# Attention with a gated FFN: new due times and engines for the first pair's rotary steps

## The chip, the cores and the metric

The kernel runs on one core of a Trainium2 chip. The metric is device time in microseconds (us) of one execution. Five engines matter here: TensorE (PE in the profile, with PEld for its weight loads), VectorE (DVE), ScalarE (ACT), GpSimd (POOL) and SyncE (SP), which here only issues DMAs. Each engine works through its own instructions strictly in the order in which the program lists them.

## The reference, cut to what matters

q, k and v have 8 batches, 8 heads, 576 positions and 64 features, all float32.

```python
q_rot, k_rot = rotate(q), rotate(k)        # x1*cos - x2*sin, x1*sin + x2*cos
scores = scale * q_rot @ k_rot.T           # scale = 1/8
attn = exp(scores - max) / (sum + 1e-9)
x = (attn @ v) with the heads side by side # (8, 576, 512)
gate = sigmoid(causal 5-tap convolution of x, one filter per channel)
out = (gate * (x @ w_val)) @ w_out
```

## The kernel before

The work goes by pairs of heads, 32 pairs in all. The host lays q and k out as [pair, 128, 2, 576]: 128 partitions are two heads of 64 features, the middle axis holds the features and the features with their halves swapped. With a table of cosines and signed sines in the same layout (`tab`, two planes), the rotation of a pair is two multiplications (`rope_mul`, plane 0 and plane 1, L211) and an addition (`rope_add`, L215). The result is then split into a rounded high part (`qk_hi`, a copy on ScalarE, L222) and a low part (`qk_lo`, a subtraction, L226), because the score matmuls (`s_mm`, L254) form each product from three partial products. Scores go to PSUM (three buffers), `s_max` (VectorE, L260) takes the row maximum and `s_exp` (ScalarE, L273) the exponential; transposes, the product with v, the convolution and, for every four pairs, the FFN follow.

The first pair alone is cut along the positions: the keys into 0 to 287 (steps with suffix `_0`) and 288 to 575 (`_1`), the queries into 0 to 255 (`_0`) and 256 to 575 (`_1`). The table is loaded in two halves on ScalarE's DMA queue (`ltab`) and each half is multiplied in place by the root of the score scale (`stab`, ScalarE, L207). The halves of k and q are loaded on SP's queue (`loadk`, `loadq`). `k_front` (ScalarE, L189) copies the last 64 keys, which lie in key half `_1`, in front of the first; every score matmul of a pair but the very first instruction comes behind it.

The convolution weights (`taps`) and the FFN weights arrive as 64-bit patterns and are decoded on the chip. `load_weight` brings four chunks of w_val (`lval0` to `lval3`, 512 KB each) on SP's queue; the decode of a chunk (`dval`) begins on VectorE with the TENSOR_SCALAR of L488.

The order of everything is written by a planner. Each step is added as a job with a due time (a base written in the code plus the entry of `DUE` under the step's key), an engine (`PICK` where there is a choice: V VectorE, G GpSimd, A ScalarE), and the names that it reads and writes. `Plan.order` takes the jobs off a heap, always the one with the lowest due time among those whose predecessors are already placed; a job whose rotating buffer is not yet free in the order is put off until the buffer's last user is placed. The order that comes out is the order of the instructions on each engine and each DMA queue; due times have no other effect. Predecessors follow from the names, in the order in which the jobs were added: a reader comes behind the last writer, and a writer behind the earlier writer and its readers. Each load of q or k also writes the name `seqk` or `seqq`, and `mul0` reads it:

```python
at(f"load{n}{fx}", ..., load, p, n, "ENGINE", a, b,
   w=toks(f"i{n}/{p}#@.@", R2, half) + f" seq{n}")
("mul0", 0, rope_mul, (0,), th + f" seq{n}", x0)
due = (16 + 12 * c) if n == "val" else (62 + 10 * c)
at(f"l{n}{c}", due - 6, "SP", 560, load_weight, n, c, ...)
```

The input buffer `iq` of the queries exists once (`"iq": 1` in `BUFS`), that of the keys twice. Pair 1's query load (`loadqe`, base -0.5, entry -1778.49, due -1778.99) therefore comes in the order behind the last job that uses pair 0's queries, and on the chip SP holds it until that job is done. The four w_val chunks have the due times -734.78, -307.96, -178.92 and -115.36, pair 1's key load (`loadke`) -528.41. The first decode step of chunk 0 is due at 13.27, the first row maximum at 14.73, `k_front` at 4.51.

Of the kernel before, what the change touches and what calls it, by code (L numbers as in the profile page):

```python
# [30 lines left out]
EARLY = 5  # L31
TURNED = {}
MOVES = ((0, 0), (2, 2), (1, 1), (3, 3), (0, 2), (2, 0), (1, 3), (3, 1), (0, 1), (2, 3), (1, 0), (3, 2), (0, 3), (2, 1), (1, 2), (3, 0))
DUE = {'vz': 23.6, 'vze': 15.3, 'taps': -2600.0, 'dtap': 21.24, 'ltab_0': -3341.07, 'stab_0': -1819.26, 'loadk_0': -2600.0, 'kmul0_0': -1008.23, 'kmul1_0': -907.74, 'kadd_0': -499.77, 'khi_0': -163.55, 'klo_0': -1718.32, 'ltab_1': -2343.23, 'stab_1': -90.27, 'loadk_1': -2600.9, 'kmul0_1': -1714.63, 'kmul1_1': -812.39, 'kadd_1': -918.5, 'khi_1': -1015.64, 'klo_1': -1297.73, 'loadq_0': -2599.1, 'qmul0_0': -471.29, 'qmul1_0': -224.67, 'qadd_0': -2063.18, 'qhi_0': -359.42, 'qlo_0': -336.86, 'loadq_1': -2599.7, 'qmul0_1': -437.78, 'qmul1_1': -251.9, 'qadd_1': -1639.5, 'qhi_1': 32.69, 'qlo_1': -105.27, 'kfronte': 9.51, 'qmixede': 12.23, 'loadve': 16.06, 's0e': -227.23, 'max0e': 13.73, 'exp0e': -339.41, 'max1e': 15.46, 'exp1e': -561.74, 's1e': -344.33, 'max2e': 12.59, 'exp2e': -68.28, 'max3e': 13.07, 'exp3e': -939.79, 's2e': 11.12, 'max4e': 14.21, 'exp4e': -768.86, 'max5e': 14.15, 'exp5e': -897.98, 's3e': -336.64, 'max6e': 15.22, 'exp6e': -1153.57, 'max7e': 15.22, 'exp7e': -160.89, 's4e': 11.95, 'max8e': 13.35, 'exp8e': 15.75, 't0e': 22.72, 'c0e': -119.34, 't1e': -192.14, 'c1e': 18.09, 't2e': -1447.45, 'c2e': -237.8, 't3e': 28.76, 'c3e': -1079.21, 't4e': 24.98, 'c4e': -326.1, 't5e': 21.07, 'c5e': 21.86, 't6e': -199.47, 'c6e': 16.33, 't7e': -188.93, 'c7e': 17.61, 'th1e': -932.6, 'ch1e': -424.79, 'th3e': -807.66, 'ch3e': 13.99, 'tme': 19.16, 'cme': -847.12, 'rinve': -2264.39, 'thme': -1195.39, 'chme': -1282.4, 'rwe': -825.13, 'rre': -20.58, 'xhie': -1613.61, 'xloe': -3315.12, 'tap0e': -58.62, 'tap1e': 14.84, 'tap2e': 26.14, 'tap3e': -35.71, 'tap4e': -280.96, 'gatee': -424.87, 'lval0': -744.78, 'dval0': -2.73, 'lval1': -329.96, 'dval1': 6.46, 'lval2': -212.92, 'dval2': -10.53, 'lval3': -161.36, 'dval3': -4.26, 'lout0': 33.92, 'dout0': 41.08, 'lout1': -38.15, 'dout1': -5.83, 'lout2': -42.59, 'dout2': 2.61, 'lout3': -9.02, 'dout3': 16.46, 'loadke': -522.91, 'kmul0e': 16.57, 'kmul1e': 10.33, 'kadde': 15.77, 'khie': -323.7, 'kloe': -335.33, 'loadqe': -1778.49, 'qmul0e': 15.87, 'qmul1e': 6.44, 'qadde': -530.8, 'qhie': -1386.96, 'qloe': -2011.52, 'f00': 39.37, 'f01': 38.45, 'f02': 36.05, 'f03': 33.98, 'f04': 14.16, 'f05': 57.36, 'f06': 50.07, 'f07': 20.21, 'f10': 29.06, 'f11': 17.31, 'f12': 20.92, 'f13': 20.77, 'f14': 40.92, 'f15': 43.76, 'f16': 25.69, 'f17': 38.33, 'loadk': -1078.23, 'kmul0': 0.53, 'kmul1': 16.98, 'kadd': -1350.24, 'khi': 18.76, 'klo': -1610.53, 'loadq': -384.18, 'qmul0': 3.26, 'qmul1': 5.91, 'qadd': -2018.7, 'qhi': 8.19, 'qlo': -1896.24, 'kfront': 17.8, 'qmixed': 16.62, 'loadv': 23.64, 's0': -615.54, 'max0': 17.71, 'exp0': -2901.14, 'max1': 16.98, 'exp1': -1877.53, 's1': 17.35, 'max2': -504.2, 'exp2': -4468.42, 'max3': -344.46, 'exp3': -2348.56, 's2': 17.89, 'max4': 17.43, 'exp4': -3148.82, 'max5': 17.12, 'exp5': -1548.82, 's3': 22.04, 'max6': -77.69, 'exp6': -1871.54, 'max7': 21.82, 'exp7': -2790.26, 's4': -339.41, 'max8': 22.7, 'exp8': -2605.32, 'x0': 15.55, 'x1': 19.39, 'x2': 21.03, 'x3': 20.75, 'x4': 24.67, 'x5': 23.33, 'x6': 20.54, 'x7': 21.88, 'tm': 26.37, 'cm': -884.96, 'rinv': 24.52, 'thm': -933.16, 'chm': -631.93, 'rw': -292.37, 'rr': 24.36, 'xhi': 31.16, 'xlo': -4576.9, 'tap0': -2383.93, 'tap1': 26.15, 'tap2': 28.12, 'tap3': 36.14, 'tap4': -411.6, 'gate': -891.23, 't0': -262.54, 'c0': -1691.36, 't1': 42.76, 'c1': -434.49, 't2': 25.32, 'c2': -1718.62, 't3': 53.27, 'c3': -1358.42, 't4': 39.43, 'c4': -1278.08, 't5': 34.66, 'c5': -3353.58, 't6': -89.01, 'c6': -675.93, 't7': -232.42, 'c7': -1808.92, 'th1': 22.4, 'ch1': -864.1, 'th3': 46.92, 'ch3': -1180.05, 'xhil0': -2099.68, 'xlol0': -375.24, 'tap0l0': -3628.89, 'tap1l0': -1727.91, 'tap2l0': -1835.19, 'tap3l0': 181.47, 'tap4l0': 25.55, 'gatel0': -1023.25, 'xhil1': -1503.17, 'xlol1': -696.91, 'tap0l1': 954.61, 'tap1l1': 2571.53, 'tap2l1': -1071.34, 'tap3l1': 218.81, 'tap4l1': -58.41, 'gatel1': 414.9, 'f0l0': 601.52, 'f0l1': 248.77, 'f0l2': 448.04, 'f0l3': 1347.11, 'f0l4': 3027.31, 'f0l5': 1209.45, 'f0l6': 1634.95, 'f0l7': 2882.08, 'f1l0': 2032.44, 'f1l1': 1849.05, 'f1l2': 2008.04, 'f1l3': 2721.13, 'f1l4': 736.1, 'f1l5': 2035.76, 'f1l6': 2263.47, 'f1l7': 2942.03, 'radd': -1399.39, 'radde': -3366.0, 'pv4': 26.64, 'pv0': -908.13, 'pv1': -175.08, 'norm0': 25.62, 'norm1': 24.65, 'pv4e': 18.34, 'pv0e': -1035.51, 'pv1e': -955.08, 'norm0e': -288.7, 'norm1e': -243.61, 'mv0': 26.57, 'mv1': -544.07, 'mv2': -117.24, 'mv3': -97.41, 'mv0e': 0.0, 'mv1e': 0.0, 'mv2e': 0.0, 'mv3e': 0.0}
PICK = {'c0': 'A', 'c0e': 'A', 'c1': 'V', 'c1e': 'V', 'c2': 'A', 'c2e': 'A', 'c3': 'V', 'c3e': 'A', 'c4': 'A', 'c4e': 'V', 'c5': 'V', 'c5e': 'A', 'c6': 'A', 'c6e': 'V', 'c7': 'V', 'c7e': 'A', 'ch0': 'A', 'ch0e': 'V', 'ch1': 'V', 'ch1e': 'A', 'chm': 'A', 'chme': 'A', 'cm': 'A', 'cme': 'A', 'kadd': 'G', 'kadd_0': 'V', 'kadd_1': 'V', 'kadde': 'V', 'kfront': 'A', 'kfronte': 'A', 'klo': 'G', 'klo_0': 'V', 'klo_1': 'V', 'kloe': 'G', 'kmul0': 'G', 'kmul0_0': 'V', 'kmul0_1': 'V', 'kmul0e': 'V', 'kmul1': 'V', 'kmul1_0': 'G', 'kmul1_1': 'V', 'kmul1e': 'G', 'od0': 'A', 'od0l': 'A', 'od1': 'A', 'od1l': 'V', 'od2': 'A', 'od2l': 'V', 'od3': 'A', 'od3l': 'A', 'qadd': 'G', 'qadd_0': 'V', 'qadd_1': 'V', 'qadde': 'V', 'qlo': 'G', 'qlo_0': 'V', 'qlo_1': 'G', 'qloe': 'G', 'qmixed': 'A', 'qmixede': 'A', 'qmul0': 'G', 'qmul0_0': 'G', 'qmul0_1': 'V', 'qmul0e': 'V', 'qmul1': 'G', 'qmul1_0': 'V', 'qmul1_1': 'V', 'qmul1e': 'G', 'xlo': 'G', 'xloe': 'G', 'xlol0': 'G', 'xlol1': 'G', 'ylo': 'G', 'ylol': 'V', 'ch3': 'A', 'ch3e': 'V', 'decout': 'A', 'decval': 'A', 'odma': 'SP', 'odmal': 'SP', 'loadk': 'SP', 'loadk_0': 'SP', 'loadk_1': 'SP', 'loadke': 'SP', 'loadq': 'SP', 'loadq_0': 'SP', 'loadq_1': 'SP', 'loadqe': 'SP', 'loadv': 'SP', 'loadve': 'SP', 'mv0': 'SP', 'mv1': 'SP', 'mv2': 'SP', 'mv3': 'SP', 'rr': 'SP', 'rre': 'SP', 'rw': 'SP', 'rwe': 'SP'}


class Plan:
# [105 lines left out]
def attn_gated_ffn(ctx: ExitStack, tc: tile.TileContext, q2, k2, v2, tab, w_val, conv_w, w_out, out, collect=None):  # L144
# [402 lines left out]
    def at(key, base, e, ns, fn, *args, pick=None, r="", w="", kb=0, mode=None, port=False):  # L547

        options = ns if pick else None
        if pick:  # L550
            e = PICK.get(pick, e)
            ns, port = options[e]
            args = [ENG[e] if a == "ENGINE" else a for a in args]
        plan.add(base + DUE.get(key, 0.0), e, fn, *args, r=r, w=w, port=port)
        if collect is not None:
# [237 lines left out]
```

## Time and profile before

| what | value |
|---|---|
| median of 3 runs | 659.55 us (659.51 to 661.09) |
| profiled execution, its own time | 661.04 us |
| span of the profiled execution | 658.9 us |
| PE busy | 611.4 us (93%) |
| DVE busy | 579.8 us (88%) |
| ACT busy | 459.5 us (70%) |
| POOL busy | 397.0 us (60%) |
| mean granted TensorE clock | 0.997 |

The span runs from the first to the last instruction of the profiled execution; its own time is 2.1 us longer, and 1.5 us above the median of the runs. All starts in the rows below count from the start of the span. POOL's durations are rough.

### The profile page before, as it was taken

The page shows a single profiled execution, that of the slowest core. Times are in us where ns is not written, and L with a number is a line of the kernel's source. Part 1 is how long each engine was busy: PE and PEld are TensorE (multiplying, and loading weights), DVE is VectorE, ACT ScalarE, POOL GpSimd, SP SyncE. Part 2 cuts the span into 40 slices and gives each one's busy share as a digit, 9 for nine tenths or more (in the row PEclk, how much of TensorE's full clock was granted, in tenths as well). Part 3 has the DMA queues.
Part 4 walks back from the last instruction along what each step waited for, and adds up shares of the span by engine and source line. Part 5 has one row for each costly group of instructions (what it writes and reads, how often), then busy time and mean ns, then how long its engine had stood idle before and what let it go on. Part 6 is the DMA issues. An engine that isn't in the chain of part 4 may idle for free.

```text
span 658.9 us, 15153 instructions
## 1 busy us (share of the span) xinstructions
PE 611.4 (93%) x5592; PEld 495.5 (75%) x5592; DVE 579.8 (88%) x830; ACT 459.5 (70%) x1152; POOL 397.0 (60%) x303
## 2 busy tenths in 40 slices
PE   1889888889989999999999999999999999999897
PEld 1666665578777887888788887888788877888696
DVE  5799988898899999999999999999999999984552
ACT  3677878677677677777787777777777777774421
POOL 2323346568577868687787768786967776630210
PEclk9999999899999999999999999999999999999999
DMA  7314432259999899899999999989999898774101
GB/s 276 123 57 143 142 128 98 96 153 264 267 246 265 232 260 244 224 277 236 267 247 256 248 272 255 264 236 264 240 260 265 221 265 248 200 178 116 38 27 63
DMA packets 51480, 134.40 MB, mean 204 GB/s; under 512 B 10928, under 2 KB 20944, under 8 KB 51408
## 3 DMA queue, kind: packets, MB, share of 16 engines
q1 hardware_dynamic: 50864, 132.86, 72.5%
q8 instruction: 44, 0.72, 0.5%
q10 hardware_dynamic: 544, 0.59, 0.3%
q14 instruction: 28, 0.23, 0.1%
HBM read 62.48 MB, written 9.59 MB: 109 GB/s over the span
## 4 chain that ended last, share of the span: by engine, by line
PE 75%; DVE 14%; ACT 5%; DMA 2%; issue 1%; SPq 1%; POOL 1%; DVEq 0%; ACTq 0%
PE ps_t L454 27%; PE ps_s L254 19%; PE ps_t L368 17%; DVE nm L260 4%; PE ps_t L358 3%; DVE big L288 2%; PE ps_t L373 2%; PE ps_t L329 2%; ACT p L273 2%; PE ps_t L302 2%; DVE g L428 1%; DMA ik<-in_k 1%; DVE big L191 1%; DMA big<-big 1%; SPq L293 1%
## 5 line engine op out<-in xcount | busy, mean ns | idle before, releaser
L273 ACT ACTIVATE p<-ps_s,nm 128x576 f32<-128x576 f32 x256 | 187.9, 738 | 78.9 <-DVE nm L260 77.8
L260 DVE TENSOR_REDUCE nm<-ps_s 128x1 f32<-128x576 f32 x288 | 202.1, 743 | 21.1 <-PE ps_s L254 20.5
L254 PE MATMUL ps_s<-k,q 64*128 64x288 f32 x1536 | 146.1, 314 | 20.8 <-ACT k L222 9.3
L254 PEld LDWEIGHTS ps_s<-k,q 64*128 64x128 f32 x1536 | 113.2, 188 | 44.7 <-issue 13.5
L288 DVE STREAM_TRANSPOSE big<-p 128x1152 f32<-128x1152 f32 x104 | 139.8, 1353 | 0.0
L428 DVE SCALAR_TENSOR_TENSOR g<-x,cw,g 128x576 f32<-128x576 f32 (+1 forms) x132 | 121.1, 917 | 2.1 <-ACT g L425 0.6
L368 PE MATMUL ps_t<-big,v 128*64 128x256 f32 (+2 forms) x1024 | 118.6, 384 | 0.0
L368 PEld LDWEIGHTS ps_t<-big,v 128*64 128x64 f32 x1024 | 70.9, 138 | 46.2 <-issue 15.1
L211 POOL TENSOR_TENSOR iq<-iq,tab 128x576 f32<-128x576 f32 (+1 forms) x59 | 84.3, 1443 | 29.7 <-DMA iq<-in_q 25.3
L215 POOL TENSOR_TENSOR ik<-ik 128x576 f32<-128x576 f32 x27 | 38.9, 1440 | 76.9 <-DVE ik L211 74.7
L454 PE MATMUL ps_t<-xh,wval_hi 128*128 128x288 f32 x256 | 78.3, 306 | 2.7 <-DVE g L459 2.0
L454 PE MATMUL ps_t<-yh,wout_hi 128*128 128x288 f32 x256 | 78.4, 306 | 1.1 <-ACT yh L463 1.1
L226 POOL TENSOR_TENSOR k<-ik,k 128x576 fp32r<-128x576 f32 x31 | 55.2, 1782 | 35.9 <-ACT k L222 34.8
L454 PE MATMUL ps_t<-yl,wout_hi 128*128 128x288 f32 x256 | 75.9, 296 | 0.1
L454 PE MATMUL ps_t<-xh,wval_lo 128*128 128x288 f32 x256 | 75.9, 297 | 0.0
L454 PE MATMUL ps_t<-yh,wout_lo 128*128 128x288 f32 x256 | 75.3, 294 | 0.0
L454 PE MATMUL ps_t<-xl,wval_hi 128*128 128x288 f32 x256 | 75.3, 294 | 0.0
L467 POOL TENSOR_TENSOR yl<-g,yh 128x288 fp32r<-128x288 f32 x56 | 45.8, 823 | 32.6 <-DVE g L428 25.2
L415 POOL TENSOR_TENSOR xl<-x,xh 128x576 fp32r<-128x576 f32 (+1 forms) x33 | 48.2, 1462 | 25.6 <-ACT xh L411 16.2
L226 POOL TENSOR_TENSOR q<-iq,q 128x576 fp32r<-128x576 f32 (+1 forms) x32 | 45.4, 1419 | 15.9 <-ACT q L222 15.8
L454 PEld LDWEIGHTS ps_t<-xh,wval_hi 128*128 128x128 f32 x256 | 48.1, 188 | 6.2 <-issue 2.6
L211 POOL TENSOR_TENSOR ik<-ik,tab 128x576 f32<-128x576 f32 (+1 forms) x32 | 45.5, 1421 | 11.5 <-DVE big L490 7.0
(91 smaller groups left out, 1072.2 us busy)
## 6 DMA issues: line engine op xcount, KB each, us to landing
big<-big SPq DMA_DIRECT2D x416, 144.0 KB
ik<-in_k SPq DMA_DIRECT2D x31, 576.0 KB
iq<-in_q SPq DMA_DIRECT2D x31, 576.0 KB
v<-in_v SPq DMA_DIRECT2D x32, 320.0 KB
rb<-rd SPq DMA_DIRECT2D x64, 144.0 KB
out_t<-oo SPq DMA_DIRECT2D x64, 144.0 KB
big<-in_w_val SPq DMA_DIRECT2D x4, 512.0 KB
big<-in_w_out SPq DMA_DIRECT2D x4, 512.0 KB
```

The lines of the kernel that those rows point to most:

```text
L211: eng.tensor_tensor(out=t[:, i, a:b], in0=t[:, i, a:b], in1=tabs[:, i, a:b], op=ALU.mult)
L215: eng.tensor_tensor(out=t[:, 0], in0=t[:, 0], in1=t[:, 1], op=ALU.add)
L226: eng.tensor_tensor(out=t[:, 1], in0=state[p][n + "in"][:, 0, a:b], in1=t[:, 0].bitcast(F32), op=ALU.subtract)
L254: T.matmul(out=ps[:, half, 0:288], lhsT=st["q"][rows, x, c * 128:c * 128 + 128] if c < 4 else mixq[p % 2][:, x], rhs=st["k"][rows, y, k0:k ...
L260: V.tensor_reduce(out=st[f"nm{i}"], in_=st[f"s{i}"], axis=AX.XY, op=ALU.max, negate=True)
L273: A.activation(out=pd.rearrange("p (b x) -> p b x", b=2), in_=st[f"s{i}"], func=AF.Exp, bias=st[f"nm{i}"], scale=1.0, accum_out=sums[p % 2 ...
L288: V.transpose(out=t[:, :, cs.index(c)].rearrange("p b k i -> p k b i"), in_=st[f"p{c}"].rearrange("p h s -> p (h s)").rearrange("p (k b i) ...
L368: T.matmul(out=acc[HEAD[h], 0:n], lhsT=st["v"][:, j, h, :], rhs=st["pt"][:, :, c0:c1, 5 * place(p, 2 * c0 + h) + j].rearrange("p a c i -> ...
L415: eng.tensor_tensor(out=st["xl"][:, a:b], in0=xs[p % 2][:, 4 + a:4 + b], in1=st["xh"][:, a:b].bitcast(F32), op=ALU.subtract)
L428: V.scalar_tensor_tensor(out=g, in0=x_sb[:, a + k:b + k], scalar=w, in1=g, op0=ALU.mult, op1=ALU.add)
L454: T.matmul(out=acc[:, 0:n], lhsT=wt[w][:, kc, ds], rhs=mv, start=(kc == 0 and i == 0), stop=(kc == NCH - 1 and i == 2))
L467: eng.tensor_tensor(out=ffn[b, "l", dc, lo], in0=y, in1=ffn[b, "h", dc, lo].bitcast(F32), op=ALU.subtract)
```

## The change: due times and engines of the first pair

Only two tables of constants change. In `PICK`, two multiplications go from GpSimd to VectorE: `kmul1_0` and `qmul0_0`. `qlo_1` stays on GpSimd. In `DUE`, the steps of the first pair get new entries; `loadq_1` keeps its own. No instruction is added or taken away.

```diff
-DUE = {'taps': -2600.0,
+DUE = {'taps': -9901,
...
-'ltab_0': -3341.07, 'stab_0': -1819.26, 'loadk_0': -2600.0, 'kmul0_0': -1008.23, 'kmul1_0': -907.74, 'kadd_0': -499.77, 'khi_0': -163.55, 'klo_0': -1718.32,
+'ltab_0': -9870.0, 'stab_0': -9830.0, 'loadk_0': -9860.0, 'kmul0_0': -9780.0, 'kmul1_0': -9771.4, 'kadd_0': -9762.8, 'khi_0': -9754.2, 'klo_0': -9734.8,
-'ltab_1': -2343.23, 'stab_1': -90.27, 'loadk_1': -2600.9, 'kmul0_1': -1714.63, 'kmul1_1': -812.39, 'kadd_1': -918.5, 'khi_1': -1015.64, 'klo_1': -1297.73,
+'ltab_1': -9892.88, 'stab_1': -9842.88, 'loadk_1': -9902.88, 'kmul0_1': -9882.88, 'kmul1_1': -9874.28, 'kadd_1': -9865.68, 'khi_1': -9857.08, 'klo_1': -9817.68,
-'loadq_0': -2599.1, 'qmul0_0': -471.29, 'qmul1_0': -224.67, 'qadd_0': -2063.18, 'qhi_0': -359.42, 'qlo_0': -336.86,
+'loadq_0': -9880.1, 'qmul0_0': -9850.0, 'qmul1_0': -9841.4, 'qadd_0': -9832.8, 'qhi_0': -9814.2, 'qlo_0': -9804.8,
-'loadq_1': -2599.7, 'qmul0_1': -437.78, 'qmul1_1': -251.9, 'qadd_1': -1639.5, 'qhi_1': 32.69, 'qlo_1': -105.27,
+'loadq_1': -2599.7, 'qmul0_1': -9752.56, 'qmul1_1': -9733.96, 'qadd_1': -9725.36, 'qhi_1': -9716.76, 'qlo_1': -9707.36,
...
-PICK = {'kmul1_0': 'G', 'qmul0_0': 'G',
+PICK = {'kmul1_0': 'V', 'qmul0_0': 'V',
```

With the bases of the code added, the due times are these:

| step | before | after | | step | before | after |
|---|---|---|---|---|---|---|
| ltab_0 | -3441.07 | -9970 | | ltab_1 | -2440.35 | -9990 |
| stab_0 | -1919.26 | -9930 | | stab_1 | -187.39 | -9940 |
| loadk_0 | -2700.0 | -9960 | | loadk_1 | -2698.02 | -10000 |
| kmul0_0 | -1048.23 | -9820 | | kmul0_1 | -1751.75 | -9920 |
| kmul1_0 | -946.34 | -9810 | | kmul1_1 | -848.11 | -9910 |
| kadd_0 | -536.97 | -9800 | | kadd_1 | -952.82 | -9900 |
| khi_0 | -199.35 | -9790 | | khi_1 | -1048.56 | -9890 |
| klo_0 | -1753.52 | -9770 | | klo_1 | -1330.05 | -9850 |
| loadq_0 | -2699.0 | -9980 | | loadq_1 | -2697.04 | -2697.04 |
| qmul0_0 | -501.29 | -9880 | | qmul0_1 | -465.22 | -9780 |
| qmul1_0 | -253.27 | -9870 | | qmul1_1 | -277.94 | -9760 |
| qadd_0 | -2090.38 | -9860 | | qadd_1 | -1664.14 | -9750 |
| qhi_0 | -385.22 | -9840 | | qhi_1 | 9.45 | -9740 |
| qlo_0 | -362.06 | -9830 | | qlo_1 | -127.91 | -9730 |
| taps | -2649.0 | -9950 | | | | |

## Rows read from the trace of the kernel before

**Rows 1.** Busy time by stretch: us, PE, PEld, DVE, ACT, POOL, granted clock, DMA share, GB/s

```profile
0.00:12.50 12.50, 0.61 (x1) 0.28 (x1) 5.95 (x18) 4.33 (x8) 2.33 (x8) 1.00 0.86 307
```

**Rows 2.** Instructions in order of time, first halves: start, duration, engine, line [idle <-releaser]

```profile
4.33 0.68 ACT L207 ACTIVATE tab<-tab 128x576 f32<-128x576 f32 x1 [1.33 <-DMA tab<-in_tab]
...
6.63 0.46 DVE L215 TENSOR_TENSOR ik<-ik 128x288 f32<-128x288 f32 x1 [0.91 <-POOL ik L211]
7.01 0.42 DVE L211 TENSOR_TENSOR iq<-iq,tab 128x256 f32<-128x256 f32 x1
7.17 0.84 POOL L211 TENSOR_TENSOR iq<-iq,tab 128x256 f32<-128x256 f32 x1 [0.57 <-DVE ik L215]
...
8.50 0.41 ACT L222 CAST q<-iq 128x256 fp32r<-128x256 f32 x1 [3.49 <-DVE iq L215]
...
9.15 0.68 ACT L207 ACTIVATE tab<-tab 128x576 f32<-128x576 f32 x1
```

**Rows 3.** Instructions in order of time, second halves and first scores

```profile
9.86 0.83 DVE L211 TENSOR_TENSOR ik<-ik,tab 128x288 f32<-128x288 f32 x2
10.72 0.46 DVE L215 TENSOR_TENSOR ik<-ik 128x288 f32<-128x288 f32 x1
11.21 0.43 ACT L222 CAST k<-ik 128x288 fp32r<-128x288 f32 x1 [1.39 <-DVE ik L215]
11.68 0.46 DVE L226 TENSOR_TENSOR k<-ik,k 128x288 fp32r<-128x288 f32 x1 [0.50 <-ACT k L222]
12.05 0.89 DVE L211 TENSOR_TENSOR iq<-iq,tab 128x320 f32<-128x320 f32 x2
12.17 0.30 ACT L189 CAST k<-k 128x128 fp32r<-128x128 f32 x1 [0.53 <-DVE k L226]
...
12.52 1.81 PE L254 MATMUL ps_s<-k,q 64*128 64x288 f32 x12 [2.62 <-ACT k L189]
12.97 0.49 DVE L215 TENSOR_TENSOR iq<-iq 128x320 f32<-128x320 f32 x1
13.38 0.42 DVE L488 TENSOR_SCALAR big<-big 128x512 int32<-128x512 int32 x1
13.50 0.46 ACT L222 CAST q<-iq 128x320 fp32r<-128x320 f32 x1 [1.03 <-DVE iq L215]
14.04 0.86 POOL L226 TENSOR_TENSOR q<-iq,q 128x320 fp32r<-128x320 f32 x1 [6.03 <-ACT q L222]
14.13 0.76 DVE L260 TENSOR_REDUCE nm<-ps_s 128x1 f32<-128x576 f32 x1 [0.33 <-PE ps_s L254]
```

**Rows 4.** SP's DMA issues in order of time

```profile
3.59 0.60 SPq L518 DMA_DIRECT2D big<-in_w_val  x1
...
14.93 0.33 SPq L197 DMA_DIRECT2D iq<-in_q  x1
15.30 0.43 SPq L197 DMA_DIRECT2D ik<-in_k  x1
```

**Rows 5.** DMA queues until 5.50 us (q1 SP, q10 ACT): packets, MB, engines' share

```profile
q10 hardware_dynamic: 544, 0.59, 38.0%
q1 hardware_dynamic: 438, 0.46, 23.7%
```

**Rows 6.** The same view, SP's queue, from 14.50 to 18.00 us

```profile
q1 hardware_dynamic: 141, 0.61, 53.3%
```

**Rows 7.** The same view, SP's queue, from 14.50 to 19.20 us

```profile
q1 hardware_dynamic: 258, 1.11, 65.3%
```

**Rows 8.** Instructions in order of time, pair 1's first rotary steps

```profile
18.69 0.75 DVE L211 TENSOR_TENSOR ik<-ik,tab 128x576 f32<-128x576 f32 x1
18.95 1.75 POOL L211 TENSOR_TENSOR iq<-iq,tab 128x576 f32<-128x576 f32 x1 [2.20 <-DMA iq<-in_q]
```

**Rows 9.** Chain that ended last, its two longest later transfers: start, us, what

```profile
274.62 4.56 DMA big<-big
...
543.14 4.28 DMA ik<-in_k
```

## What the change does to the time: the prediction

> **What bounds the kernel now.** I read the busy time by stretch first. Over the whole kernel TensorE sets the pace, but the change touches only the start, and there TensorE hardly works: 0.61 of the first 12.5 us [rows 1]. What is worth anything there is whatever lets the first scores and the first row maxima begin, because from then on pair follows pair and a later start moves everything behind it. I then read the order of instructions up to the first maximum. The reader should see two chains. The keys' second half sets the scores: its multiplications at 9.86, then addition, high part, low part, `k_front` at 12.17, scores at 12.52. It had to wait until ScalarE reached the second half of the table at 9.15, behind the casts of the first halves [rows 2, 3]. VectorE sets the first maximum: the decode of w_val's chunk 0 (L488) stands ahead of it, starts at 13.38 straight behind the last rotary addition, and the maximum follows at 14.13, 0.33 after the decode step for TensorE's sake [rows 3]. So L488 waited for nothing: w_val had been issued at 3.59 [rows 4].
>
> Last I read SP's queue. Pair 1's query load goes out at 14.93, just after GpSimd has finished pair 0's last query step (14.04 and 0.86); the key load behind it goes at 15.30, although that buffer's last user, the keys' low part, had ended at 12.14 [rows 3, 4]. A load that waits for its buffer holds what SP has behind it. In the kernel before, all four w_val chunks were already out by then.
>
> **The order that the new due times give.** The words of the change want key half `_1` first. Reading the planner's rule for `seqk`, `loadk_1` writes a name that `kmul0_0` has read, so it is placed only after `kmul0_0`; likewise `loadq_1` behind `qmul0_0`. Its due time of -10000 can't help. Taking the lowest due time that is ready, step by step:
>
> - ScalarE: both table loads (`_1` first), both scalings, high parts of query `_0`, key `_1`, key `_0`, query `_1`, then `k_front` (4.51), which before stood ahead of query `_1` (9.45).
> - VectorE: query `_0` whole; `kmul0_0`; key `_1` whole; the rest of key `_0`; query `_1` up to its addition; then L488, then the maximum, as before.
> - SP: `loadq_0`, `loadk_0`, taps, `loadk_1`, `loadq_1`; then pair 1's query load (-1778.99), and only behind it w_val chunk 0 (-734.78), pair 1's keys (-528.41), chunks 1 to 3. Before, `qhi_1` at 9.45 kept the query buffer in use past all of w_val's due times; now -9740 and -9730 free it in the plan first. The taps stay third.
>
> Reading the kernel before by the same rule gives the order that its trace shows: w_val at 3.59, and pair 1's query load behind all its chunks [rows 4]. That is why I trust it.
>
> **The cost, step by step.**
>
> 1. Table. Both scalings come on landing, which removes the stand of the second one until 9.15. But the first VectorE step now needs the table half that lands second. ScalarE's queue has all of its 544 packets at 5.50 at the latest [rows 5]; the first half's scaling began at 4.33, 0.68 long [rows 2]. I take 5.60 for the second scaling and 6.30 for the first multiplication.
>
> By the Trainium skill (DMA: Bandwidth & Descriptors, Queues, rings and completion order) a DMA engine takes turns between the queues it has work for, packet by packet. The rows show 544 packets of ScalarE's queue against 438 of SP's, so the turns are not even here [rows 5]; even turns would let 106 more packets (0.11 MB, 0.27 us at the rate of step 5) go first, and the sum would be 0.27 higher. I keep the rows.
>
> 2. Query `_0` (256 wide). Two multiplications, now both on VectorE: 2 x 0.42 less an overlap of 0.06, 0.78. The addition at most 0.46 as for 288 [rows 2], the cast 0.41 and 0.04 to the next, then the low part; from the start of a low part to the next multiplication takes 0.37 (11.68 to 12.05) [rows 2, 3]. Together 2.06: 8.36. What this removes is GpSimd's 0.84 and the like with their handoffs (0.91 and 0.57 of waiting) [rows 2]; it is inside the chain, since all of it now runs on one engine.
>
> 3. Keys. From [rows 3], start to start: pair of multiplications to addition 0.86, addition to cast 0.49, cast to low part 0.47, low part to next 0.37. Three multiplications in a row are 1.29, so key `_1`'s addition is at 9.65, cast 10.14, low part 10.61. Then one multiplication (0.46 and 0.03) at 10.98, addition 11.47, cast 11.96, low part 12.43. VectorE idles at each cast, because nothing else stands between.
>
> 4. Query `_1` at 12.80: multiplications to addition 0.92, to cast 0.53, to GpSimd's low part 0.54 [rows 3]: cast at 14.25, GpSimd from 14.79 to 15.65. `k_front` now waits for the cast's 0.46 and starts at 14.73; the scores 0.35 later at 15.08, against 12.52: 2.56 late.
>
> 5. SP. Pair 1's query load goes out 0.03 after GpSimd, at 15.68, and w_val chunk 0 behind it on the same queue. In the trace that load went at 14.93 and its reader could start at 18.95, 4.02 later [rows 4, 8]. Between 18.00 and 19.20 the queue moved 1.11 - 0.61 = 0.50 MB, 0.417 MB a us [rows 6, 7]. Chunk 0 is 0.524 MB: 1.26 more. So L488 can start at 15.68 + 4.02 + 1.26 = 20.96. The lower bound by bytes alone: both together are 0.590 + 0.524 = 1.114 MB, which had moved 4.27 after the issue (at 19.20) [rows 4, 7]; that gives 19.95. I take the upper value, since the reader of the query load also started about a us after its bytes had gone by.
>
> 6. VectorE waits in front of L488 from about 14.2 on, and behind it stand all row maxima. The scores of the first query block are ready at 16.7 and fill two of three buffers; nothing else can move. Maximum 0 starts 0.42 after 20.96, at 21.38, against 14.13: **7.25 us late**.
>
> Further: pair 1's keys land 0.59 MB or 1.4 us behind chunk 0, at 22.4; their multiplication on VectorE at 18.69 [rows 8] moves to 25.9, so 3.5 us cover it, and without that cover the loss would grow by what exceeds it. Chunks 1 to 3 follow at 1.3 us each, ahead of a decode that takes several VectorE steps per chunk. GpSimd's wait of 2.20 for the queries [rows 8] disappears, but its multiplication was not what the scores of pair 0 waited for: nothing. The other terms of the change (taps, lows on VectorE) cost nothing apart from their place in the chain. From the first maximum on, order and work are the same, so I count the delay as rigid.
>
> Sum against the profiled execution: 661.04 + 7.25 = 668.3; it lies 1.5 above the median, which goes to 659.55 + 7.25 = 666.8. Its bounds: 1.0 less for step 5, 0.3 less where the table lands sooner; 0.3 more for even turns and up to 0.9 more for a late straggler of a transfer, as long as the lag of step 5. So 665.5 to 668.0.
>
> **The rivals.**
>
> A. *w_val is not held.* If SP issued w_val ahead of the held query load, L488 would find its data, and the price is step 4's alone: 2.56, so 662.1. For it: the trace of before has just that order. Against it: the due times. 7 in 100.
>
> B. *The words come true.* If `loadk_1` really went first, key `_1` would start at about 5.2 after a first scaling at 4.33, and the VectorE chain (15 steps of 0.40 to 0.46, 6.4, and one stall of 0.4) would put `qhi_1` near 12.0 and GpSimd's end near 13.4; w_val would still be held behind the query load: L488 at 13.4 + 5.3 = 18.7, 4.9 late with the maximum, 664.4. Against it: `seqk`. 6 in 100.
>
> C. *The loss is given back* (the other side). The chain that ended last has two long transfers, 4.56 and 4.28 [rows 9]. If these began by a clock of their own and not by what computes, a later start would eat into them, up to 8.84. From 5.3 us given back the change is within the noise: 657.9 to 661.5. Against it: loads and moves are issued when buffers come free or data is made, and so move along. 7 in 100, 2 of them faster.
>
> D. *The hold goes on.* If chunk 1 or pair 1's keys arrive late as well, VectorE waits a second time, for 2 to 4 us: 669 to 671. The cover of 3.5 above speaks against it. 6 in 100.
>
> **How the numbers follow.** A measurement here tells 0.3%, 2.0 us, from no change. My forecast, 666.8, has 74 in 100. The range of 663.8 to 668.8 holds nearly all of it (its own bounds, and the runs' spread upward), and B; it leaves out A, C and D, about 2 in 10 with the edges. Faster: 0.02 from C. The same: 0.05 from C and 0.01 where A comes out short. Slower: the rest, 0.92.
>
> **What would show it.** Right: SP issues pair 1's query load near 15.7 with w_val behind it; L488 idles some 6 us for w_val and starts near 21; scores start near 15.1 with `k_front` behind the query cast; distance between maximum 0 and the end as before. Wrong: w_val issued in the first 7 us (A); a key load ahead of the query load on SP (B); the delay of the first maximum larger than that of the end (C), or another wait on DMA behind 22 us (D). What I may have misread is the planner's order; every large term hangs on it.

## The result, and the profile after

The kernel became slower. Over 18 runs each, the medians are 668.57 us after (663.17 to 673.90) and 661.05 before (657.74 to 668.78); the ratio is 1.0094, with a 95% interval from 1.0069 to 1.0119, which is 6.2 us (4.6 to 7.9). Two of the 18 runs after (673.20 and 673.90) are left out of the ratio as slow ones, over 1.5% above the fastest; the median of the other 16 is 667.75. The span of the profiled execution went from 658.9 to 666.1, 7.2 more. The three runs before that the prediction was set against had a median 1.5 below that of the eighteen.

Instructions in order of time up to the first maximum, of the kernel after, in the same columns as [rows 2, 3]:

```profile
5.80 0.68 ACT L207 ACTIVATE tab<-tab 128x576 f32<-128x576 f32 x1 [0.89 <-DMA tab<-in_tab]
6.52 0.76 DVE L211 TENSOR_TENSOR iq<-iq,tab 128x256 f32<-128x256 f32 x2 [4.24 <-ACT tab L207]
...
8.55 1.19 DVE L211 TENSOR_TENSOR ik<-ik,tab 128x288 f32<-128x288 f32 x3
9.78 0.46 DVE L215 TENSOR_TENSOR ik<-ik 128x288 f32<-128x288 f32 x1
...
14.37 0.46 ACT L222 CAST q<-iq 128x320 fp32r<-128x320 f32 x1 [1.85 <-DVE iq L215]
14.74 0.29 ACT L189 CAST k<-k 128x128 fp32r<-128x128 f32 x1
14.91 0.87 POOL L226 TENSOR_TENSOR q<-iq,q 128x320 fp32r<-128x320 f32 x1 [13.60 <-ACT q L222]
...
15.08 1.81 PE L254 MATMUL ps_s<-k,q 64*128 64x288 f32 x12 [1.91 <-ACT k L189]
...
20.90 0.43 DVE L488 TENSOR_SCALAR big<-big 128x512 int32<-128x512 int32 x1 [6.56 <-DMA big<-in_w_val]
21.24 0.75 DVE L260 TENSOR_REDUCE nm<-ps_s 128x1 f32<-128x576 f32 x1
```

The last two rows are the result in short: VectorE sits idle for 6.56 us, released by the load of w_val, and the first row maximum comes at 21.24 instead of 14.13 [rows 3], 7.11 late. The scores, begun at 15.08, had been there since about 16.7 (they take 1.6 until the maximum can start, as in [rows 3]); VectorE does not take the maximum ahead of L488, which the program lists first. The front copy of the keys (L189) stands right behind the query cast on ScalarE.

Why w_val is late stands in SP's issues, of the kernel after, in the columns of [rows 4] (the 12.55 of the third row spans two loads, query half 1 and the held one of pair 1), and in its waits up to 18 us (what waited, for whom, us in total, times, longest):

```profile
0.74 0.69 SPq L197 DMA_DIRECT2D iq<-in_q  x1
1.48 0.82 SPq L197 DMA_DIRECT2D ik<-in_k  x1
...
3.59 12.55 SPq L197 DMA_DIRECT2D iq<-in_q  x2
16.18 0.43 SPq L518 DMA_DIRECT2D big<-in_w_val  x1
16.66 0.43 SPq L197 DMA_DIRECT2D ik<-in_k  x1
```

```profile
SPq L197 <- POOL q L226: 7.4, 1, 7.4
SPq L197 <- DMA iq<-in_q: 4.1, 1, 4.1
```

SP stood before pair 1's query load for 11.5 us, first for the landing of the last query half into the same buffer, then for GpSimd's last step on it. Chunk 0 of w_val went out 12.59 later than before (16.18 against 3.59).

### The profile page after: what moved, and what is told of

Its sections match the earlier page's. It is cut to its first block, busy times and chain, and to the rows that moved or that the text cites. A ratio compares the mean times of both kernels' runs of the same rounds, so it can differ in the third digit from the quotient of the medians.

```text
span 666.1 us, 15150 instructions
## 1 busy us (share of the span) xinstructions
PE 611.7 (92%) x5592; PEld 496.9 (75%) x5592; DVE 579.7 (87%) x832; ACT 460.4 (69%) x1152; POOL 396.0 (59%) x301
## 4 chain that ended last, share of the span: by engine, by line
PE 71%; DVE 16%; ACT 5%; DMA 4%; issue 2%; SPq 2%; POOL 1%; ACTq 0%; DVEq 0%; POOLq 0%
PE ps_t L454 27%; PE ps_s L254 18%; PE ps_t L368 15%; DVE nm L260 5%; DVE big L288 3%; PE ps_t L358 3%; PE ps_t L329 2%; PE ps_t L302 2%; PE ps_t L373 2%; DVE g L428 2%; SPq L293 2%; ACT p L273 2%; DMA ik<-in_k 1%; DVE big L191 1%; DMA big<-big 1%
## 5 line engine op out<-in xcount | busy, mean ns | idle before, releaser
L211 POOL TENSOR_TENSOR iq<-iq,tab 128x576 f32<-128x576 f32 x58 | 83.1, 1449 | 29.5 <-DMA iq<-in_q 23.9
L211 POOL TENSOR_TENSOR ik<-ik,tab 128x576 f32<-128x576 f32 x31 | 44.5, 1436 | 13.1 <-DMA ik<-in_k 6.6
```

The source lines that it names most:

```text
L211: eng.tensor_tensor(out=t[:, i, a:b], in0=t[:, i, a:b], in1=tabs[:, i, a:b], op=ALU.mult)
```

## The experiments

The time of the first maximum is read off one profile each; it repeats well (14.13 and 14.08 in two profiles of the kernel before). Ratios are to runs of the kernel before on the same chip, with their 95% intervals. Apart from experiment 2, the spans of the single profiles came out 1.7 to 8.3 us longer than expected wherever a figure or a range was named: 663.2, 658.0, 669.0, 666.2, 659.8, 661.5 and 669.7 for experiments 1 to 7, 662.5 for 9 and for 10. Executions of one kernel differ by as much (657.74 to 668.78 for the kernel before), so the ends are read off the runs.

**1. Chunk 0 ahead of the held load.**

```diff
 # changed kernel
-'lval0': -744.78
+'lval0': -2010.0
```

> The changed kernel with one entry altered: the load of w_val's chunk 0 gets an earlier due time, so that SP issues it before pair 1's query load instead of behind it. If the held load is what costs the most (my theory), L488 no longer waits for w_val: it starts near 14.3 as soon as the last rotary addition is done, the first maximum follows the first scores at about 16.7 instead of 21.24, and the span falls from 666.1 to about 661.5 (2.5 above before: what is left is the front copy of the keys behind the query cast). Rival: the wait only moves, because pair 1's keys and the other chunks still stand behind the held load; then VectorE waits a second time and the span stays above 664.

Instructions in order of time of this kernel:

```profile
14.20 0.42 DVE L488 TENSOR_SCALAR big<-big 128x512 int32<-128x512 int32 x1
...
15.02 1.81 PE L254 MATMUL ps_s<-k,q 64*128 64x288 f32 x12 [1.91 <-ACT k L189]
...
16.63 0.76 DVE L260 TENSOR_REDUCE nm<-ps_s 128x1 f32<-128x576 f32 x1 [2.02 <-PE ps_s L254]
```

L488 no longer waits for anything, and the maximum now waits for the scores: 16.63, 4.6 sooner than in the changed kernel, 2.50 later than before. The ratio is 1.0061 (1.0038 to 1.0085), the span 663.2; I had expected 661.5. So lifting the hold alone gives back 4.6 of the 7.1 at the first maximum; the other 2.5 is the later scores, which the wait for w_val had covered. The rival's second wait did not come: from 17 to 56 us VectorE waited for TensorE alone. By the runs the kernel is 4.0 us behind before (2.5 to 5.6), so the 2.5 left at the first maximum lies only at the edge of what they allow; where the rest comes from stays open.

**2. The second query half's casts late again.**

```diff
 # changed kernel
-'qhi_1': -9716.76, 'qlo_1': -9707.36
+'qhi_1': 32.69, 'qlo_1': -105.27
```

> The changed kernel with two entries put back to their old values: high part and low part of the first pair's second query half. This puts the front copy of the keys ahead of the query cast on ScalarE again, and pair 1's query load behind all of w_val on SP. If these two places are the whole loss, the scores start near 12.9, L488 near 14.3, the first maximum near 14.75, and the span is 659.5, half a us above before. Rival: the new order on VectorE (query half first, the key halves one after the other) costs most of it by itself; then the first maximum stays above 16 and the span above 661.

Instructions in order of time of this kernel:

```profile
12.37 0.29 ACT L189 CAST k<-k 128x128 fp32r<-128x128 f32 x1
...
12.51 2.30 PE L254 MATMUL ps_s<-k,q 64*128 64x288 f32 x13 [12.51 <-ACT k L222]
...
14.61 0.76 DVE L260 TENSOR_REDUCE nm<-ps_s 128x1 f32<-128x576 f32 x1
```

Two entries put back undo nearly all: first maximum at 14.61, 0.48 late; ratio 1.0017 (0.9993 to 1.0042), no difference. The new order on VectorE costs no more than this 0.48.

**3. The same two entries alone, in the kernel before.**

```diff
 # kernel before
-'qhi_1': 32.69, 'qlo_1': -105.27
+'qhi_1': -9716.76, 'qlo_1': -9707.36
```

> The kernel before with only the two new entries of the second query half's high and low part. ScalarE then casts that half ahead of the front copy of the keys; on SP pair 1's query load goes ahead of w_val's chunks 2 and 3, but chunk 0 stays early. Theory: L488 stays near 13.4, the front copy moves from 12.17 to about 14.0, scores near 14.35, the first maximum near 15.95, 1.8 late, span 660.7. Rival: the held load delays L488 or a later decode step here as well; then the first maximum or the next decode chunk waits for a transfer and the span is above 662.

Instructions in order of time of this kernel:

```profile
13.32 0.42 DVE L488 TENSOR_SCALAR big<-big 128x512 int32<-128x512 int32 x1
...
13.80 0.29 ACT L189 CAST k<-k 128x128 fp32r<-128x128 f32 x1
...
15.23 0.91 SPq L518 DMA_DIRECT2D big<-in_w_val  x2
15.76 0.76 DVE L260 TENSOR_REDUCE nm<-ps_s 128x1 f32<-128x576 f32 x1 [2.02 <-PE ps_s L254]
```

Here only chunks 2 and 3 of w_val go behind the held load, and L488 keeps its place; the front copy behind the query cast alone makes the first maximum 1.63 late (15.76). Ratio 1.0030 (0.9995 to 1.0066), which holds this loss (1.0025) but also no change. The profile taken with it was one of the longest, 669.0, and tells nothing of the end.

**4. Loads of the first pair ordered by half.**

```diff
 # changed kernel
-toks(f"i{n}/{p}#@.@", R2, half) + f" seq{n}"
+toks(f"i{n}/{p}#@.@", R2, half) + f" seq{n}{half[0] if first else ''}"
...
-th + f" seq{n}"
+th + f" seq{n}{half[0] if first else ''}"
```

> The changed kernel with the name that orders the loads split by half for the first pair, so that the load of key half 1 no longer stands behind the multiplication of key half 0: the change as its words have it. My theory: key half 1 starts near 5.2 and the rotary steps end about 1.9 us sooner than in the changed kernel, but w_val is still behind the held query load, so L488 starts near 18.8, the first maximum near 19.15, 5.0 after that of before, span 663.9. Rival: with the intended order the change is a gain, the span is below 659.

Instructions in order of time of this kernel:

```profile
4.95 0.83 DVE L211 TENSOR_TENSOR ik<-ik,tab 128x288 f32<-128x288 f32 x2 [2.67 <-DMA ik<-in_k]
...
11.64 0.49 DVE L215 TENSOR_TENSOR iq<-iq 128x320 f32<-128x320 f32 x1
...
18.62 0.43 DVE L488 TENSOR_SCALAR big<-big 128x512 int32<-128x512 int32 x1 [6.49 <-DMA big<-in_w_val]
18.96 0.75 DVE L260 TENSOR_REDUCE nm<-ps_s 128x1 f32<-128x576 f32 x1
```

With the key half that holds the last 64 keys truly first, VectorE is through 2.2 sooner (the last addition starts at 11.64 instead of 13.85), and then waits 6.49 for w_val all the same. First maximum 4.83 late, ratio 1.0069 (1.0046 to 1.0092). The intended order alone is no gain over the kernel before; against the changed kernel it gives back 2.28 at the first maximum.

**5. Both: loads by half, casts late.** The edits of 2 and 4 together.

> Both edits together: the loads of the first pair ordered by half, and the second query half's high and low part with their old due times. Nothing is held on SP and the front copy goes ahead of the query cast. Theory: scores from about 11.0, L488 near 12.2, the first maximum near 12.65, 1.5 before that of the kernel before, span 657.4. Rival: w_val's chunk 0 or another transfer then lands too late for the earlier chain and the first maximum stays at 14 or later, span 659.

Instructions in order of time of this kernel:

```profile
12.17 0.42 DVE L488 TENSOR_SCALAR big<-big 128x512 int32<-128x512 int32 x1
...
12.58 0.76 DVE L260 TENSOR_REDUCE nm<-ps_s 128x1 f32<-128x576 f32 x1
```

The first maximum is 1.55 earlier than before, as expected. The runs don't show it: ratio 0.9997 (0.9971 to 1.0022), which still holds a gain of 1.55 (0.9977).

**6. The engine part alone.**

```diff
 # kernel before
-'kmul1_0': 'G', 'qmul0_0': 'G'
+'kmul1_0': 'V', 'qmul0_0': 'V'
```

> The kernel before with only the two multiplications moved from GpSimd to VectorE. Theory: the two waits of VectorE on GpSimd (0.91 and 0.61) go and two multiplications (0.43 and 0.40) come instead: everything up to the first maximum starts 0.7 sooner, which lies at 13.4, span 658.2. Rival: VectorE is the longer chain, the added work costs 0.8 and the first maximum is at 14.9 or later.

Instructions in order of time of this kernel:

```profile
12.69 0.42 DVE L488 TENSOR_SCALAR big<-big 128x512 int32<-128x512 int32 x1
...
13.44 0.76 DVE L260 TENSOR_REDUCE nm<-ps_s 128x1 f32<-128x576 f32 x1 [0.33 <-PE ps_s L254]
```

The part that moves the two multiplications gains 0.69 at the first maximum. The runs say 1.0028 (0.9995 to 1.0062), whose interval doesn't hold that gain; nothing in the first 20 us explains it, and it stays open.

**7. Chunk 0 one place further back.**

```diff
 # changed kernel
-'lval0': -744.78
+'lval0': -410.0
```

> The changed kernel with w_val's chunk 0 one place further back on SP, behind pair 1's key load too. Theory: 0.59 MB more go ahead of it, 1.4 us at 0.417 MB a us: L488 starts near 22.3 instead of 20.90, the first maximum near 22.65, span 667.5. Rival: L488 does not wait for its place in the queue but for a fixed completion; then it stays within 0.3 of 20.9.

Instructions in order of time of this kernel:

```profile
20.79 1.40 POOL L211 TENSOR_TENSOR ik<-ik,tab 128x576 f32<-128x576 f32 x1 [5.15 <-DMA ik<-in_k]
22.06 0.43 DVE L488 TENSOR_SCALAR big<-big 128x512 int32<-128x512 int32 x1 [7.86 <-DMA big<-in_w_val]
22.41 0.75 DVE L260 TENSOR_REDUCE nm<-ps_s 128x1 f32<-128x576 f32 x1
```

Its rotary steps ran 0.13 sooner than in the changed kernel; L488 came 1.16 later, so 0.59 MB more in front cost 1.3, where 1.4 was expected. The first maximum is 8.28 late and the ratio 1.0137 (1.0102 to 1.0172), 9.1 us (6.8 to 11.4): the place in SP's queue sets the time.

**8. The kernel before once more.**

> The kernel before, unchanged, profiled a second time. Both theories: the first maximum within 0.1 of 14.13. What differs in the span from 658.9 is what one execution differs from another, and no edit's effect.

First maximum at 14.08, span 660.1. What differs is in the last section.

**9 and 10. Matmuls in front.** Six extra matmuls on zeros ahead of the first scores in the kernel before, and five in the kernel of experiment 5; nothing reads what they write.

```diff
+warm = psum.tile([128, 512], F32, name="ps_t0", tag="ps_t0", bufs=1)
+for _ in range(6):
+    T.matmul(out=warm, lhsT=ident, rhs=pm[:, 0:512], start=True, stop=True)
```

> The kernel before with six extra matmuls of 128x512 on zeros into an unused PSUM buffer, from about 1.8 us on, before the first scores; their result is never read. It asks what the executions differ by: in two profiles of the kernel before, twelve score matmuls take 1.81 us up to about 24, later 1.05, and the change to the faster rate came at 24 in one and at 28 in the other, with the first product with v 2.5 us apart. Theory: the slow rate is left over from TensorE's idle start; work there brings the fast rate to the first scores, the first product with v comes 2 to 4 us before 39.48, span 655 to 657. Rival: the waits between 14 and 24 (up to 1.5 each) bring the slow rate back, or the rate has nothing to do with the work before; then the first twelve score matmuls still take 1.8 and the span stays at 659.

> The changed kernel with its loads ordered by half and the second query half's casts late (first maximum at 12.58), with five such extra matmuls in front. Theory: both gains add, 1.5 from the earlier first maximum and 2 to 4 from the faster matmuls, span 654 to 656, and the runs tell it from before. Rival: as above, or the extra matmuls last beyond 10.5 and push the first scores back; then the span is 658 or more.

Busy time of TensorE by stretch in experiment 9 (us, busy, granted clock, DMA share, GB/s):

```profile
0.00:4.00 4.00, 2.26 (x3) 1.00 0.42 122
4.00:8.00 4.00, 4.00 (x9) 1.00 1.08 384
8.00:10.00 2.00, 1.06 (x3) 1.00 1.07 399
10.00:12.00 2.00, 0.00 (x0) 0.92 1.01 405
12.00:14.00 2.00, 1.67 (x12) 0.50 1.03 414
14.00:28.00 14.00, 10.91 (x51) 0.50 0.25 85
```

What the rival foresaw came, but not for its reason. The extra work got faster (0.75 us a recorded matmul up to 4 us, 0.44 in the next four), then the engine stood idle for most of 8.7 to 12.3, and from about 12 to 28 us the granted clock was 0.50: the fast rate was gone before the scores began, and not by the waits between 14 and 24. The first twelve score matmuls took 1.81 again, and the first product with v began at 39.30 instead of 39.48. Experiment 9 has its first maximum at 13.95 and a ratio of 0.9990 (0.9960 to 1.0019), no difference; experiment 10 has its first maximum at 12.35 and 0.9972 (0.9946 to 0.9999). By the runs it is the only version whose whole interval lies ahead of the kernel before, by 1.9 us, and only just.

## Why the prediction was right

**The order.** Right in every place. SP held w_val behind pair 1's query load, `loadk_1` did not go first (SP's first load is a query half, where experiment 4 has a key half at 0.74), and `k_front` stood behind the query cast. Experiment 4 shows that the planner's name for the loads was what kept the key half back; experiment 2 that the new places of `qhi_1` and `qlo_1` carry nearly all of the loss. They do so only together with the other new due times: alone in the kernel before they cost 1.63 at the first maximum (experiment 3), because chunk 0 still goes out ahead of the held load there.

**Steps 1 to 4.** The second scaling began at 5.80 instead of 5.60, and everything on VectorE ran 0.1 to 0.2 later than worked out, with nearly the same distances: key addition 9.78 (9.65), query cast 14.37 (14.25), GpSimd's end 15.78 (15.65). Scores at 15.08, to the hundredth, and that was luck: the cast came 0.12 late, but `k_front` began 0.37 after the cast's start instead of the 0.48 counted. ScalarE's queue again had all its 544 packets by 5.50, against 429 of SP's (544 to 438 before [rows 5]). Such totals do not test the rule of the Trainium skill weighed there, that a DMA engine takes turns between its queues packet by packet (DMA: Bandwidth & Descriptors, Queues, rings and completion order). SP's queue had moved only 6 packets by 3.50, when ScalarE's had moved 222, and from 3.50 to 5.50 it moved 423 against ScalarE's 322. Whether both queues had work all that time no row shows, so the prediction's reading that the turns were not even is not shown. The 0.2 is not that rule's 0.27 either way: ScalarE's last packet was over by 5.38, earlier than the 5.50 counted, and the scaling began 0.42 behind it.

**Steps 5 and 6.** The chain of work that ended last, first 25 us of the kernel after (start, us, what):

```profile
14.91 0.88 POOL q L226
...
15.80 0.33 SPq L197
...
16.18 4.69 DMA big<-in_w_val
...
20.90 0.43 DVE big L488
21.33 0.68 DVE nm L260
```

L488 at 20.90 (20.96), the maximum at 21.24 (21.38), so 7.11 late where 7.25 was forecast. The rate and the lag that were read off two loads of the kernel before held for w_val to within 0.2: from the issue of the held load to L488 it took 5.10 where 5.28 was counted. Issued 0.12 later than forecast, it made L488 0.06 early, so two small errors cancel in part.

**The cover.** GpSimd's multiplication of pair 1's keys waited for its load until 22.38 (22.4 forecast), and VectorE's began at 25.80 (25.9): no second wait, rival D did not come. From 22 to 60 us VectorE waited for TensorE alone.

**Rigid from there on.** The span grew by 7.2, the runs by 6.2 (4.6 to 7.9). That the 7.1 of the first maximum stands again in the span is in part luck. Against the first profile of the kernel before, the 288 row maxima of the kernel after come between 4.6 and 8.0 late, the last one 7.1. The second profile of the kernel before (experiment 8) itself lies between 3.2 early and 2.8 late of the first, and against it the span grew by 6.0. So single profiles show a rigid delay only to within some 3 us, and the runs to within their interval. Rival C is out for the changed kernel: at most 2.5 can have been given back. Over the experiments, the shift of the first maximum, from 1.78 early to 8.28 late, lies inside the interval of the runs for seven of the nine timed ones, at its edge for experiment 1 and outside it for experiment 6. Rivals A and B were built as experiments 1 and 4: 2.50 at the first maximum for A (2.56 forecast), 4.83 for B (4.9).

**The level.** 668.57 lies just inside the range of 663.8 to 668.8, but above the 665.5 to 668.0 that the sum's own bounds gave. The kernel before itself has a median of 661.05 over more runs, not 659.55, and 661.05 + 7.25 would have been 668.3. The difference was forecast well; that the level stayed inside as well rests on the room left for the runs' spread.

## What to carry to other kernels

A load that must wait for its buffer can stop its whole queue, as it did on SP here for 11.5 us, so a step that frees a buffer earlier in the plan can bring that load ahead of others which needed no wait: look at what a due time lets out, not only at the step it belongs to. Read the order rule before the due times; a name that two loads share can outweigh any number. And when two steps on an engine change places, ask which of them the next engine is waiting for: 1.6 us went on one cast ahead of a copy of 0.3.

## What the runs showed of the hardware that was not expected

In the profiles without extra matmuls TensorE runs its score matmuls at half rate from the start until some moment between about 22 and 37 us, and that moment differs between executions of one kernel. The first product with v in two profiles of the kernel before, matmuls in order of time, first the one of [rows 3] and then experiment 8:

```profile
22.49 0.60 PE L254 MATMUL ps_s<-k,q 64*128 64x288 f32 x1
24.33 1.81 PE L254 MATMUL ps_s<-k,q 64*128 64x288 f32 x11 [1.23 <-ACT p L273]
...
39.48 0.66 PE L358 MATMUL ps_t<-big,v 64*64 64x256 f32 x8
```

```profile
22.45 0.50 PE L254 MATMUL ps_s<-k,q 64*128 64x288 f32 x1
24.28 1.05 PE L254 MATMUL ps_s<-k,q 64*128 64x288 f32 x11 [1.34 <-ACT p L273]
...
36.91 0.81 PE L358 MATMUL ps_t<-big,v 64*64 64x256 f32 x8
```

The same eleven matmuls take 1.81 in the one and 1.05 in the other, at the same place, after the same work; the product with v is 2.57 apart. The granted clock of the profile reads 1.00 in both stretches, so here the durations tell the level (1.2 against 2.4 GHz), not that column. In experiment 7 eleven matmuls still took 1.80 at 32.60, and the fast rate was there at 36.95. The 2.57 did not last: the execution that was ahead here has the longer span, by 1.2 us.

A second place where the level differs lies some 120 us later, where TensorE idles for 2.0 us. Matmuls behind that idle time, first in the kernel before, then in the kernel after:

```profile
145.79 0.40 PE L454 MATMUL ps_t<-xh,wval_hi 128*128 128x288 f32 x1 [2.02 <-DVE g L459]
...
147.87 1.06 PE L254 MATMUL ps_s<-k,q 64*128 64x288 f32 x12
```

```profile
151.68 0.40 PE L454 MATMUL ps_t<-xh,wval_hi 128*128 128x288 f32 x1 [2.01 <-DVE g L459]
...
154.35 1.79 PE L254 MATMUL ps_s<-k,q 64*128 64x288 f32 x12
```

The granted clock was 0.50 from 153 to 156 in the kernel after, and stayed at 1.00 in the kernel before. The row maxima of the two were 5.9 apart in front of this place and 7.2 behind it. The idle time is the same 2.0 in all twelve profiles. In five of them the granted clock fell to 0.50 within 2 us of its end (the kernel after and experiments 2, 4, 5 and 10), and the row maxima behind it came 1.2 to 1.4 later than those in front of it, both against the first profile of the kernel before; in the other six the difference was 0.02 at most. So a fall there costs about 1.3 us, and it came in some profiles and not in others; what decides it no run shows. Such places are as large as most edits here. They are a part of the spread of the runs (657.7 to 668.8 for the kernel before); how much of it they make, no experiment isolated.
